# A plain last unit, earlier global values, and filler products of a constant tile in an attention and mixture-of-experts kernel

## The chip, the core and the metric

The kernel runs on one core of one Trainium2 chip. A core has a matrix engine (TensorE, PE in the profile; PEld is its weight load), a vector engine (VectorE, DVE), a scalar engine (ScalarE, ACT), a general engine (GpSimd, POOL), a queue that only issues transfers (SyncE, SP), and 16 DMA engines that move data between memory (DRAM) and the on-chip memories: SBUF for operands, PSUM for the matrix engine's results. Each engine works through its own instructions in order and waits on semaphores for the others. The metric is the time of one execution on the device in microseconds (us); lower is better.

## What is computed

First an attention over 8 batches of 8 heads with 512 local and 32 global positions of 64 values each. Global queries see all positions; local queries see the global positions and a band of 32 to each side. Then a mixture of experts over the 4352 resulting rows of 512: the logits of 8 experts go through 8 rounds of row and column scaling, and every row goes through every expert.

```python
    s_g = scale * np.matmul(q_g, k_all.transpose(0, 1, 3, 2))
    out_g = np.matmul(sm(s_g), v_all)
    ...
    s_l = np.concatenate([s_lg, s_ll], axis=-1)          # s_ll masked to |i - j| <= 32
    out_l = np.matmul(sm(s_l), np.concatenate([v_g, v_l], axis=2))
    ...
    for e in range(E):
        h = np.maximum(x @ w1[e], 0.0)
        ye = h @ w2[e]
        out += P[:, e:e + 1] * ye
```

## The kernel before

The whole program is one function, and the order of instructions on each engine is the order in which the function calls them (the schedule is manual). It has three stretches that matter here.

**The head (about 0 to 21 us).** Lines 269 to 319 load what the first batch needs. POOL issues, in this order: qs and ks of heads 2 and 3 (L174, from load_qk), four mask instructions (L310), qs and ks of heads 4 to 7 (L174), then load_v(0): the cast of the global values, cast_vg(0) (L183), which writes v_g[0] as 16-bit numbers to the DRAM tile vg16[0]; the local values va in four loads (L193, and L196 three times) and vb in one (L200). Then come cast_vg(1) (L183) and clear_z(0) (L297, L298, L300, L301), which clears the tile vgz[0], writes a column of it, and prepares vgn. SP issues load_vz(0): four loads from vg16[0] into vgz[0] (L180), each with 32 rows, and a fifth into vgn (L319). A vgz load must wait for the cast to land and for the clear. The local values are needed twice, in va and shifted in vb; for the first two batches POOL makes vb by copies (function part, L204 to L209), issued in slot 1.

**The slots.** A loop over s (L562 on) runs one slot for each of 32 pairs of heads, two heads a slot. Slot s makes the scores of pair s in three parts (st_B: PE L368, or L372 and L375 later; VectorE L379 masks and takes the minimum, ScalarE L382 the exponential), transposes the weights of pair s-1 (st_D1 L389, st_D2 L403; the copies to SBUF are VectorE's L391 and ScalarE's pg, L405), transposes the queries and keys of pair s+1 (st_A: PE L332; VectorE copies the keys into kTe, four tiles in turn, L336; ScalarE copies the queries, L337), and multiplies the weights by the values (st_E: PE L423, which reads va, vb and vgz; VectorE L427 and L428 divide and so release the PSUM tile). st_E(0) stands in slot 2, st_E(1) and st_E(2) in slot 3, and st_E(s-1) in slot s after that. Even slots from 2 on make scores of global queries (st_G1, L455), odd ones from 3 on use them (L468, L481, L494, L497). From slot 5 on the same loop also runs the first expert products of experts 0 and 1 (PE ph L523, py L537), four and two pieces a slot. In slots 1 to 4, where there is no such piece yet, keep_busy(3) follows st_A: three products of the identity with the first 512 columns of kTe[0], whose result nobody reads (L553). kTe[0] is written by st_A(0), and again by st_A(4) in slot 3.

**The experts.** Experts 2 to 7 use Strassen's scheme with seven products of half size in place of eight. The second layer works in units of 256 rows. A Strassen unit has four sums of its inputs (sums, L867, 128x512 each), seven products m1 to m7 (mm, L871, four matmuls of 256 columns each) on a PSUM tile z of four quarters (two such tiles exist), two ScalarE copies within z (L885 behind m1, L892 behind m6), and three VectorE reads into the output rows (read, L905): r2 after m4 and m5, r7, and r1 after m3. A plain unit (function plain) has 16 matmuls of 512 columns (L940) in two halves and two VectorE reads (L943); plain(u, last, between) runs the functions in between ahead of given matmuls, keyed by half and place; with last true the second half is split in three pieces of columns. Its results are in tiles of the PSUM pools mm and sc. store issues the output rows on SP (L833).

The end of the program has four units u0 to u3 behind the last Strassen unit x of the loop:

```python
        u1.sums()
        plain(u0, False, {(0, FT - 2): (x.m3, x.r1, lambda: u2.sums(nc.gpsimd)), (1, 3): (u1.m1,)})
        for w in (u1.m7, u1.m2, u1.m6, u2.m1, u1.m4, u1.m5, u1.r2, u1.r7, u2.m7, u2.m2, u2.m6, u1.m3, u1.r1):
            w()
        plain(u3, True, {(0, 3): (u2.m4, u2.m5, u2.r2, u2.r7), (0, FT - 2): (u2.m3, u2.r1)})
```

So u1 and u2 are Strassen units, u0 and u3 plain ones; u1's sums are VectorE's and u2's GpSimd's.

Of the kernel before, what the change touches and what calls it, by code (L numbers as in the profile page):

```python
# [10 lines left out]
FP16 = mybir.dt.float16  # L11
# [12 lines left out]
def kernel(  # L24
# [13 lines left out]
    nc = tc.nc  # L38
# [5 lines left out]
    P = 128  # L44
# [8 lines left out]
    FT = F // P  # L53
# [15 lines left out]
    ones_f = persist.tile([P, P], FP32)  # L69
    identity = persist.tile([P, P], FP16)  # L70
# [58 lines left out]
    with ExitStack() as att:  # L129
# [12 lines left out]
        kTe = [att_c.tile([P, KC * W], FP16, name=f"kTe{i}") for i in range(4)]  # L142
# [9 lines left out]
        def natural(b):  # L152
            return b < 2
# [18 lines left out]
        def load_qk(b, *hs):  # L172
            staged[b] = tuple(att_in.tile([P, H, NJ, Dh], FP16, tag=t, name=t) for t in ("qs", "ks"))
            return [lambda t=t, src=src, h0=h0, h1=h1: nc.gpsimd.dma_start(  # L174
                        out=t[:, h0:h1], in_=src[b, h0:h1].rearrange("h (p s) d -> p h s d", s=NJ))
                    for h0, h1 in zip(hs, hs[1:]) for t, src in zip(staged[b], (q_l, k_l))]

        def load_vz(b):
            for i in range(4):
                nc.sync.dma_start(out=vgz[b % 2][i:P:4, i, :, 0:Dh], in_=vg16[b])  # L180

        def cast_vg(b):
            nc.gpsimd.dma_start(out=vg16[b], in_=v_g[b].rearrange("h g d -> g h d"))  # L183

        def load_v(b):
            va, vb = vab[b % 2]
            vz = vgz[b % 2]
            src = v_l[b].rearrange("h s d -> s h d")

            def first():  # L190
                if b != 1:
                    cast_vg(b)
                nc.gpsimd.dma_start(out=va[W:P, 0, :, 0:Dh], in_=src[0:96])  # L193

            def mid(j):
                nc.gpsimd.dma_start(out=va[:, j, :, 0:Dh], in_=src[P * j - W : P * j + 96])  # L196

            def last():
                r = HB if natural(b) else W
                nc.gpsimd.dma_start(out=vb[r : r + W, NJ - 1, :, 0:Dh], in_=src[Sl - W : Sl])  # L200

            def part(eng, lo):
                if lo:
                    eng.tensor_copy(out=vb[96:P, NJ - 1], in_=va[W : 2 * W, 0])  # L204
                    eng.tensor_copy(out=vb[0:HB, 0:2], in_=va[HB:P, 0:2])
                    eng.tensor_copy(out=vb[0:HB, 2:NJ], in_=va[HB:P, 2:NJ])
                else:
                    eng.tensor_copy(out=vb[HB:P, 0:2], in_=va[0:HB, 1:3])
                    eng.tensor_copy(out=vb[HB:P, 2], in_=va[0:HB, 3])  # L209

            def move():
                if natural(b):
                    return part
                nc.sync.dma_start(out=vb[96:P, NJ - 1], in_=va[W : 2 * W, 0])
                nc.sync.dma_start(out=vb[0:W, :], in_=va[HB : HB + W, :])
                nc.sync.dma_start(out=vb[HB : HB + W, :], in_=va[HB + W : P, :])
                nc.sync.dma_start(out=vb[W:HB, 0 : NJ - 1], in_=va[0:W, 1:NJ])
                nc.sync.dma_start(out=vb[HB + W : P, 0 : NJ - 1], in_=va[W:HB, 1:NJ])
                load_vz(b)

            return [first] + [lambda j=j: mid(j) for j in range(1, NJ)] + [last, move]
# [38 lines left out]
        def run(steps):  # L260
            for f in steps:
                f()
# [14 lines left out]
        steps = load_qk(0, 2, 4, H)  # L277
# [18 lines left out]
        def clear_z(i, eng):  # L296
            eng.memset(vgr[i].bitcast(mybir.dt.uint32), 0)  # L297
            eng.tensor_copy(out=vgz[i][:, :, :, Dh], in_=own.unsqueeze(2).to_broadcast([P, 4, H]))  # L298
            if i == 0:
                eng.memset(vgn[0 : P - Sg], 0.0)  # L300
                eng.memset(vgn[P - Sg : P, :, Dh:VW], 1.0)  # L301
# [5 lines left out]
        for a in range(2):  # L307
            band = mask[HB * a : HB * (a + 1), 1, 0:KW]
            for base, m, c in ((0, -1, 1), (2 * W, 1, -1)):
                nc.gpsimd.affine_select(out=band, in_=band, compare_op=ALU.is_ge, fill=NEG, base=base,  # L310
                                        pattern=[[c, KW]], channel_multiplier=m)
        run(steps[2:4])
        *steps, move = load_v(0)
        part = move()
        run(steps)
        cast_vg(1)
        clear_z(0, nc.gpsimd)
        load_vz(0)
        nc.sync.dma_start(out=vgn[P - Sg : P, :, 0:Dh], in_=vg16[0])  # L319

        st = {}
# [227 lines left out]

        def keep_busy(n):  # L550
            pm = ps_mm.tile([P, 512], FP32, tag="mm", name="pm")
            for i in range(n):
                nc.tensor.matmul(pm, identity, kTe[0][:, 0:512], start=True, stop=True)  # L553

        queue = []
        NU = B * HP
# [13 lines left out]
        for s in range(NU + 2):  # L570
            b, hp = divmod(s, HP)
# [89 lines left out]
            if 1 <= s < 5:  # L661
                keep_busy(3)
# [98 lines left out]
    with tc.tile_pool(name="tpool", bufs=2) as tpool, \  # L761
# [68 lines left out]
        def store(m, c, eng):  # L830
            if m < B:
                r0 = S * m + Sg + P * c
                eng.dma_start(out=out[r0 : r0 + P, :], in_=ogs[m][:, c, :])  # L833
            else:
                for b in range(4 * c, 4 * c + 4):
                    eng.dma_start(out=out[S * b : S * b + Sg, :], in_=ogs[m][W * (b % 4) : W * (b % 4 + 1), c, :])
# [15 lines left out]
        class Unit:  # L852
# [6 lines left out]
            def o(self, j):  # L859
                return acc_of(self.m)[:, self.c[j], :]  # L860

            def sums(self, eng=nc.vector):
                a11, a12, a21, a22 = self.a
                s = self.s = hsum.tile([P, 3, HF, P], FP16, tag="hs", name="hs")
                for o, x, y, op in ((s[:, 1], a11, a21, ALU.subtract), (a21, a21, a22, ALU.add),
                                    (s[:, 0], a21, a11, ALU.subtract), (s[:, 2], a12, s[:, 0], ALU.subtract)):
                    eng.tensor_tensor(out=o, in0=x, in1=y, op=op)  # L867

            def mm(self, o, lhs, rhs, first):
                for fk in range(HF):  # L870
# [3 lines left out]
            def w(self, i, j):  # L874
                return w2s[self.k][:, HF * i : HF * (i + 1), H2 * j : H2 * (j + 1)]
# [55 lines left out]
        def plain(u, last, between):  # L931
            order = sorted(range(FT), key=lambda fk: (fk % HF == HF - 1, fk))
            for j in range(2):
                for d0, d1 in ((0, H2), (H2, 3 * P), (3 * P, D)) if last and j else ((0, D),):
                    pool, tag = (ps_sc, "sc") if (j + (d0 > 0)) % 2 else (ps_mm, "mm")
                    z = pool.tile([P, D], FP32, tag=tag, name="zp")
                    for n, fk in enumerate(order):
                        for f in between.get((j, n), ()) if d0 == 0 else ():
                            f()
                        nc.tensor.matmul(z[:, d0:d1], u.a[2 * j + fk // HF][:, fk % HF, :], work["last"][:, fk, d0:d1],  # L940
                                         start=(n == 0), stop=(n == FT - 1), skip_group_check=True)
                    o = u.o(j)[:, d0:d1]
                    nc.vector.scalar_tensor_tensor(out=o, in0=z[:, d0:d1], scalar=u.p[j], in1=o, op0=ALU.mult, op1=ALU.add)  # L943
                store(u.m, u.c[j], nc.sync)
# [135 lines left out]
        for k, (pas, e) in enumerate(stages):  # L1080
# [3 lines left out]
            n = len(slots)  # L1084
# [31 lines left out]
        p, x = state["slot"], state["unit"]  # L1116
        for w in (x.m4, x.m5, x.r2, x.r7, p.m4, p.m3):
            w()
        u0, u1, u2, u3 = final
        u1.sums()  # L1120
        plain(u0, False, {(0, FT - 2): (x.m3, x.r1, lambda: u2.sums(nc.gpsimd)), (1, 3): (u1.m1,)})
        for w in (u1.m7, u1.m2, u1.m6, u2.m1, u1.m4, u1.m5, u1.r2, u1.r7, u2.m7, u2.m2, u2.m6, u1.m3, u1.r1):
            w()
        plain(u3, True, {(0, 3): (u2.m4, u2.m5, u2.r2, u2.r7), (0, FT - 2): (u2.m3, u2.r1)})


# [28 lines left out]
```

## Time and profile before

| | |
|---|---|
| median of 3 runs (lowest, highest) | 996.84 us (996.23, 996.92) |
| the profiled execution, and its span | 996.39 us, 994.6 us |
| PE busy, matmuls | 978.8 us (98%), 8644 |
| VectorE busy | 776.9 us (78%) |
| ScalarE busy | 659.8 us (66%) |
| GpSimd busy | 305.2 us (31%) |
| mean granted PE clock | 0.998 |

The span runs from the first instruction of the program to the last event that the profile shows; the execution's own time is 1.8 us longer. All times of the text are from the span's start. Busy time counts each engine's instructions; PE's ends are modelled, about 0.17 us past the point at which the next matmul can start. "Idle before" in a timeline row is in brackets, with the instruction that ended it. A row of the chain of waits has its start, its length and the instruction, or "issue" where nothing that the profile shows was waited for. A row of a DMA issue gives the issuing queue; its landing is taken from the tile's view, issue by issue. The granted clock is 1.00 at full speed and 0.50 at half.

### The profile page before, as it was taken

The numbers are of one execution on the slowest core, as the hardware profiler recorded it, in microseconds if no ns is written. First come the engines' busy times: TensorE is split into PE (matmuls) and PEld (weight loads), VectorE is DVE, ScalarE is ACT, GpSimd is POOL, SyncE is SP. The second block draws the span as 40 slices with busy tenths as digits, with TensorE's granted clock in tenths as the row PEclk, the third lists the DMA queues.
The fourth block names the chain that finished last, engine by engine and source line by source line (L and its number), as shares of the span: only waits on it lengthen the run. The fifth ranks groups of instructions, "written<-read, shape, count | busy, mean of one in ns | idle before, by whom it ended". The sixth has DMA issues, their size and how long they took to land.

```text
span 994.6 us, 22109 instructions
## 1 busy us (share of the span) xinstructions
PE 978.8 (98%) x8644; PEld 637.0 (64%) x8644; DVE 776.9 (78%) x1919; ACT 659.8 (66%) x1372; POOL 305.2 (31%) x366
## 2 busy tenths in 40 slices
PE   7899999999999999999999999999999999999997
PEld 5565556555555556666666666676767676766765
DVE  7876666666663755899999888997899999888887
ACT  6898888888884566765555555557765555555551
POOL 9649887887860201111111111101111111100001
PEclk9999999999999999999999999999999999999999
DMA  9999999999952477554443333575654543123043
GB/s 165 189 163 207 226 213 212 224 203 234 225 141 85 121 229 189 161 138 118 117 106 75 75 74 75 138 212 138 160 138 118 117 116 71 38 56 73 2 106 128
DMA packets 138248, 138.65 MB, mean 139 GB/s; under 512 B 56800, under 2 KB 110240, under 8 KB 136096
## 3 DMA queue, kind: packets, MB, share of 16 engines
q0 software_dynamic: 105696, 87.32, 51.6%
q1 hardware_dynamic: 31888, 49.60, 15.7%
q8 instruction: 67, 1.10, 0.4%
q10 hardware_dynamic: 560, 0.33, 0.1%
q14 instruction: 37, 0.30, 0.1%
HBM read 144.46 MB, written 39.58 MB: 185 GB/s over the span
## 4 chain that ended last, share of the span: by engine, by line
PE 93%; DVE 2%; ACT 2%; POOL 1%; DMA 1%; issue 1%; SPq 0%; ACTq 0%; DVEq 0%; POOLq 0%
PE z L871 30%; PE pa L969 18%; PE py L537 12%; PE ph L523 11%; PE pb L969 9%; PE pc L969 4%; PE sc L375 1%; PE po L423 1%; PE ptw L389 1%; ACT Pu L382 1%; PE pk L332 1%; DMA vgz<-vg 1%; PE tgx L399 1%; PE pq L332 1%; PE sg L455 0%
## 5 line engine op out<-in xcount | busy, mean ns | idle before, releaser
L871 PEld LDWEIGHTS <-hs 128*128 128x128 f16 x2320 | 226.1, 98 | 96.1 <-issue 2.9
L871 PE MATMUL z<-w2e,hs 128*128 128x256 f16 x1336 | 200.4, 273 | 2.3 <-DVE o L905 1.0
L871 PE MATMUL z<-v,hs 128*128 128x256 f16 x984 | 147.6, 273 | 0.0
L892 ACT COPY z<-z 128x256 f32<-128x256 f32 x100 | 35.7, 357 | 145.9 <-PE z L871 145.9
L523 PE MATMUL ph<-xT,w1e 128*128 128x512 f16 (+1 forms) x576 | 130.2, 367 | 0.6 <-ACT xT L407 0.6
L537 PE MATMUL py<-w2e,hT 128*128 128x512 f16 x544 | 128.2, 379 | 0.0
L382 ACT ACTIVATE Pu<-ms,mx 128x160 f16<-128x160 f32 x256 | 119.6, 637 | 11.7 <-DVE mx L379 9.6
L969 PEld LDWEIGHTS <-w1e 128*128 128x128 f16 x960 | 87.1, 98 | 51.6 <-issue 1.0
L969 PE MATMUL pa<-t,s 128*128 128x512 f16 x384 | 114.2, 379 | 0.0
L787 POOL DMA_DIRECT2D w1e<-in_moe_w_dram x24 | 17.4, 733 | 290.7 <-PE pa L969 220.4
L379 DVE CUSTOM_DVE_ANT_0 ms<-sc,mask 128x160 f32<-128x160 f32 x256 | 70.0, 320 | 46.3 <-ACT yst L540 27.6
L867 DVE TENSOR_TENSOR hs<-hs 128x512 f16<-128x512 f16 x228 | 99.1, 435 | 8.4
L905 DVE SCALAR_TENSOR_TENSOR oy<-z,lg,oy 128x512 f32<-128x512 f32 x128 | 95.8, 748 | 7.3 <-ACT oy L910 5.9
L787 POOL DMA_DIRECT2D w2e<-in_moe_w_dram x24 | 19.8, 830 | 243.6 <-PE z L871 214.2
L973 DVE CUSTOM_DVE_ANT_0 hx<-pb,s 128x512 f16<-128x512 f32 x96 | 65.9, 686 | 36.4 <-ACT s L1003 30.4
L523 PEld LDWEIGHTS <-w1e 128*128 128x128 f16 x576 | 54.5, 98 | 53.0 <-issue 1.1
L989 ACT ACTIVATE hs<-pa 128x512 f16<-128x512 f32 x96 | 57.2, 596 | 46.8 <-PE pa L969 46.8
L973 DVE CUSTOM_DVE_ANT_0 hs<-pb,s 128x512 f16<-128x512 f32 x96 | 65.8, 686 | 24.1 <-ACT s L1003 23.7
L969 PEld LDWEIGHTS <-s 128*128 128x128 f16 x720 | 65.6, 98 | 28.5 <-issue 0.3
L537 PEld LDWEIGHTS <-hT 128*128 128x128 f16 x544 | 49.9, 98 | 51.9
L528 DVE TENSOR_SCALAR hT<-ph 128x512 f16<-128x512 f32 x58 | 40.1, 691 | 50.1 <-PE ph L523 50.0
L526 ACT ACTIVATE hT<-ph 128x512 f16<-128x512 f32 (+1 forms) x86 | 50.7, 589 | 27.6 <-PE ph L523 27.1
(203 smaller groups left out, 1935.0 us busy)
## 6 DMA issues: line engine op xcount, KB each, us to landing
ys<-yd SPq DMA_DIRECT2D x68, 256.0 KB, 3.2
yd<-yst SPq DMA_DIRECT2D x16, 1024.0 KB, 6.4
pw<-in_moe_w_dram POOLq DMA_DIRECT2D x24, 512.0 KB, 10.1
kept<-psum POOLq DMA_DIRECT2D x24, 512.0 KB, 4.8
s<-kept POOLq DMA_DIRECT2D x12, 768.0 KB, 8.8
v<-kept POOLq DMA_DIRECT2D x12, 768.0 KB, 8.7
w1e<-in_moe_w_dram POOLq DMA_DIRECT2D x12, 512.0 KB, 5.4
w2e<-in_moe_w_dram POOLq DMA_DIRECT2D x12, 512.0 KB, 6.5
```

Source lines behind the costliest of these rows:

```text
L379: nc.vector.tensor_tensor_reduce(out=ms[:, ii, :], in0=sc[:, SW * ii : SW * (ii + 1)], in1=mask[:, mi, :], scale=-scale, scalar=BIG, op0=A ...
L382: nc.scalar.activation(out=d["Pu"][:, i // 4, :, i % 4], in_=ms[:, ii, :], func=AF.Exp, scale=-1.0, bias=d["mx"][:, i : i + 1])
L523: nc.tensor.matmul(ph[:, 0:n], wts[e][0][:, dk, P * fm : P * (fm + 1)], xT[:, dk, c0 : c0 + n], start=(dk == 0), stop=(dk == DP - 1))
L526: nc.scalar.activation(out=hT[:, fm, 0:n], in_=ph[:, 0:n], func=AF.Relu)
L528: nc.vector.tensor_scalar(out=hT[:, fm, 0:n], in0=ph[:, 0:n], scalar1=0.0, scalar2=None, op0=ALU.max)
L537: nc.tensor.matmul(py, hT[:, fk, P * c : P * (c + 1)], wts[e][1][:, fk, :], start=(fk == 0), stop=(fk == FT - 1))
L867: eng.tensor_tensor(out=o, in0=x, in1=y, op=op)
L871: nc.tensor.matmul(o, lhs[:, fk, :], rhs[:, fk, :], start=(first and fk == 0), stop=(fk == HF - 1), skip_group_check=True)
L905: nc.vector.scalar_tensor_tensor(out=o, in0=z, scalar=p, in1=o, op0=ALU.mult, op1=ALU.add)
L969: nc.tensor.matmul(o, lhs[:, dk, P * f : P * (f + 1)], rhs[:, dk], start=(first and n == 0 and dk == 0), stop=(dk == HD - 1), skip_group_c ...
L973: nc.vector._custom_dve(TENSOR_ADD_SAT, out=self.to(i, j), in0=self.of(ps), in1=self.of(s), s0=BIG, s1=0.0)
L989: nc.scalar.activation(out=self.to(1, 0), in_=self.of(self.pa), func=AF.Relu)
```

## The change

It has three parts.

- **The end.** u2 becomes a plain unit: its sums on GpSimd, its seven products and three reads go, and 16 matmuls of 512 columns and two reads come. u1's m4, m5, r2, r7 and its m3, r1 are now called from inside u2, and u3 has nothing between its matmuls. sums loses its parameter for the engine.
- **The start.** cast_vg(0) is issued ahead of qs and ks of heads 4 to 7, no longer in load_v(0); clear_z(0) right after the first va load, ahead of the other three; load_vz(0) ahead of cast_vg(1), which is on another queue.
- **The unread products.** keep_busy(3) issues six products of 256 columns instead of three of 512; they read ones_f, a 128x128 tile of 32-bit ones taken as 256 columns of 16-bit numbers, in place of kTe[0]. ones_f is written at the start of the program (L281, and one column by L284) and never again.

```diff
             def first():
-                if b != 1:
+                if b > 1:
                     cast_vg(b)
                 nc.gpsimd.dma_start(out=va[W:P, 0, :, 0:Dh], in_=src[0:96])
...
+        cast_vg(0)
         run(steps[2:4])
         *steps, move = load_v(0)
         part = move()
-        run(steps)
+        steps[0]()
+        clear_z(0, nc.gpsimd)
+        run(steps[1:])
+        load_vz(0)
         cast_vg(1)
-        clear_z(0, nc.gpsimd)
-        load_vz(0)
         nc.sync.dma_start(out=vgn[P - Sg : P, :, 0:Dh], in_=vg16[0])
...
         def keep_busy(n):
             pm = ps_mm.tile([P, 512], FP32, tag="mm", name="pm")
-            for i in range(n):
-                nc.tensor.matmul(pm, identity, kTe[0][:, 0:512], start=True, stop=True)
+            for i in range(2 * n):
+                nc.tensor.matmul(pm[:, 0 : 2 * P], identity, ones_f.bitcast(FP16), start=True, stop=True)
...
-            def sums(self, eng=nc.vector):
+            def sums(self):
...
-                    eng.tensor_tensor(out=o, in0=x, in1=y, op=op)
+                    nc.vector.tensor_tensor(out=o, in0=x, in1=y, op=op)
...
-        plain(u0, False, {(0, FT - 2): (x.m3, x.r1, lambda: u2.sums(nc.gpsimd)), (1, 3): (u1.m1,)})
-        for w in (u1.m7, u1.m2, u1.m6, u2.m1, u1.m4, u1.m5, u1.r2, u1.r7, u2.m7, u2.m2, u2.m6, u1.m3, u1.r1):
+        plain(u0, False, {(0, FT - 2): (x.m3, x.r1), (1, 3): (u1.m1,)})
+        for w in (u1.m7, u1.m2, u1.m6):
             w()
-        plain(u3, True, {(0, 3): (u2.m4, u2.m5, u2.r2, u2.r7), (0, FT - 2): (u2.m3, u2.r1)})
+        plain(u2, False, {(0, 3): (u1.m4, u1.m5, u1.r2, u1.r7), (1, 3): (u1.m3, u1.r1)})
+        plain(u3, True, {})
```

In the order of the built program nothing else moves. In the kernel after, lines behind L313 of before have a number higher by two, those of the last units (from about L1125) by three.

## The prediction

> **What bounds the kernel now.** I read the page first, then the chain of work that ended last at both ends of the span, then the timelines of the engines there, and last the times at which single loads landed.
>
> ```profile
> PE 978.8 (98%) x8644; PEld 637.0 (64%) x8644; DVE 776.9 (78%) x1919; ACT 659.8 (66%) x1372; POOL 305.2 (31%) x366
> ...
> PE   7899999999999999999999999999999999999997
> ```
>
> TensorE (PE) is busy 98% of the span; only the first two of 40 slices and the last one leave it room. After its idle of 0.56 us at 40.05 us its timeline up to 62 us names one gap, of 0.18 us, and the chain is nearly PE alone until 972 us. So a change pays only by starting that full stretch sooner or by shortening the end. The chain near the start (start, length, what):
>
> ```profile
> 14.61 6.71 DMA vgz<-vg
> 21.32 0.04 issue
> 21.36 0.53 PE po L423 x21
> ...
> 25.75 0.61 DVE kTe L336
> 26.36 0.04 issue
> 26.40 0.81 PE pm L553 x3
> 27.21 0.30 PE sc L368 x8
> ```
>
> The first value product of slot 2 (st_E(0), L423) stops for the fourth vgz load, and in slot 3 the unread products (keep_busy, L553) stop for VectorE's (DVE's) copy into kTe[0], which is one of their operands; the scores behind them stop too. At the end, VectorE and PE:
>
> ```profile
> 970.33 0.42 DVE L867 TENSOR_TENSOR hs<-hs,hx 128x512 f16<-128x512 f16 x1
> ...
> 976.49 4.45 DVE L867 TENSOR_TENSOR hs<-hs 128x512 f16<-128x512 f16 x4
> 980.87 0.74 DVE L905 SCALAR_TENSOR_TENSOR oy<-z,lg,oy 128x512 f32<-128x512 f32 x1
> ```
> ```profile
> 976.93 5.02 POOL L867 TENSOR_TENSOR hs<-hs 128x512 f16<-128x512 f16 x4 [29.22 <-DVE hs L867]
> ```
> ```profile
> 981.66 0.60 PE L871 MATMUL z<-w2e,hs 128*128 128x256 f16 x4 [0.97 <-DVE oy L905]
> ...
> 984.76 0.60 PE L871 MATMUL z<-w2e,hs 128*128 128x256 f16 x4 [0.32 <-DVE ox L905]
> ...
> 988.51 0.60 PE L871 MATMUL z<-w2e,hs 128*128 128x256 f16 x4 [0.98 <-DVE o L905]
> 988.94 2.36 PE L940 MATMUL zp<-w2e,hs 128*128 128x512 f16 x26
> ```
>
> Four sums on VectorE take 1.8 us at 970 us, but 4.45 us at 976 us, where GpSimd (POOL) makes u2's four sums beside them. The read behind them (r1, L905) frees the PSUM tile that u2.m1 needs, so PE stands still; it does so twice more, at u1.m3 and u2.m3, for reads that come just ahead of them.
>
> **The end, step by step.** A Strassen unit is 7 products of 4 matmuls of 256 columns; four of them take 0.435 us (1.31 us for 12 in the chain), so 7 x 0.435 = 3.05 us. A plain unit is 16 matmuls of 512 columns at 0.2165 us (0.65 us for 3 in the chain) = 3.46 us. u2 as a plain unit costs 0.41 us more on PE. What goes are the three stalls, counted from where PE could have issued: 980.10 + 0.435 = 980.54 to 981.66 is 1.12; 983.84 + 0.435 = 984.28 to 984.76 is 0.48; 986.72 + 0.65 = 987.37 to 988.51 is 1.14; together 2.74 us. Net 0.41 - 2.74 = **-2.3 us**.
>
> What is late next? u1.m6 still ends its issue at 980.54, and u2's first three matmuls follow (its PSUM buffers are long free) to 981.19. u1.m4 then waits for ScalarE's (ACT's) copy of m6's result: before, it starts 0.64 us after m6 starts and takes 0.36, so 980.10 + 1.00 = 981.10: 0.09 us to spare, the tightest place. u1.m5 ends at 982.23, r2 reads until 983.0; u1.m3, which that read releases, comes at 983.79, behind five matmuls of u2's first half and three of its second. u2 ends its issue at 985.32, u3's first half at 987.05, and its three last pieces, 1.77 us as before (991.31 - 0.17 - 989.37), at 988.82; the last result is there at 989.0 against 991.31. VectorE has u1's sums in 1.8 us (978.3), then r1, and stays ahead also if they kept their 4.45: no PE instruction that is left waits for that r1. The last L943 and store (991.34 to the span's end) follow unchanged. Bounds: -1.9 (some 0.2 us each at m4 and m3) to -2.4.
>
> **The start, step by step.** On POOL's queue vg[0]'s cast moves ahead of two loads (qs and ks of heads 4 to 7), and clear_z(0), 11.27 to 13.24, moves ahead of va's three loads, to about 7.3 to 9.25. Nothing is added, so from 13.15 on POOL stands as before; the casts and loads it is moved past are issued later: qs and ks by 0.66 us (the cast's issue), the va loads and vb by 1.95, vg[1] by 1.95. On SP's queue the four vgz loads wait for the cast's landing (before: issued 5.86, 6.6 us to landing, 12.47) and for the clear's copy (12.63); before, both end together, so both had to move. After: the loads land in order of issue, ks's first part at 7.6, so the cast at about 8; the clear's copy ends near 8.65. The vgz loads then go out at 8.7 instead of 12.65, and with the same 4.6 to 6.7 us to landing the fourth is there at about 17.4, not 21.32. The next condition of st_E(0) is vb: POOL's last copy (L209) ends at 20.57. PE starts at 20.35, so it runs through and ends near 21.1 instead of 21.89; VectorE is free at 21.14. **-0.75 us**; nothing below that, for vb holds it.
>
> The copies on POOL (L204 on, from 16.20) need va, whose last two loads landed at 14.9 and 16.0, 6.7 and 7.0 us after their issue; a small cast issued at 50.7, with little queued ahead, landed 2.3 us later. Some 4 us of that are queue, so a pause of 1.95 us in issuing is covered. If that cover is gone: L206 (17.86) may wait, and each us it waits is lost to st_E(0).
>
> keep_busy: six matmuls of 256 columns cost what three of 512 do (6 x 0.109 against 3 x 0.2165 = 0.65 us). They read a tile last written at 3.64 us, so the wait in slot 3 goes and none is added; in slots 1, 2 and 4 the row shows no wait to lose. In slot 3, with the 0.75 already won: transposes from 24.34, keep_busy from 24.91 (0.35 us after pq, as in slot 2), scores from 25.65, VectorE's next L379 at 26.14 instead of 27.63: 1.49 in all. The next limit is ScalarE's copy pg (26.41 to 26.87, now 0.75 sooner, 26.12), which st_E(2) needs: its end moves by 1.3, not 1.5. ScalarE then runs with one gap of 0.24 us from 30.5 to 40.0 and starts PE's full stretch, so **-1.3 us** carries on. The loads that do not move with it land in time: vgz[1] by 36.7 for its use near 40, w2e at 49.9 for 58. Bounds: 0 (all lost to late loads) to -1.5 (pg no limit).
>
> **Sum.** -2.3 - 1.3 = -3.6 us. The profiled execution took 996.39 (span 994.6): 992.8. The three runs' median is 0.45 above it, so I forecast **993.2**.
>
> [...] In the rows, ks lands at 12.17 and its transposes start at 13.01: 0.84 to spare. The cast ahead of it costs 0.30 (its landing behind ks's now, 12.17 to 12.47). [...]
>
> **Rivals.**
> - *Shared DMA engines eat the start* (0.15). In rows: two vgz landings are 0.50 apart (17.25, 17.75); with the cast's 0.30 ks lands up to 1.3 later, 13.47, and slot 1 up to 0.46 late: the start gives -0.8. If va is held up as well by over 1.84 us (it needs to be there at 17.86), all of the start goes: 996.84 - 2.3 = 994.5. For: the GB/s at 10 to 15 us are lower (147) than at 5 to 10 (200). Against: in 17 to 20 us, with vgz loads under way, qs and ks still land 1.5 us apart.
> - *The end gives nothing* (0.05): something holds u1.m4 or u1.m3 as long as the three stalls did; 995.5. The copy's 0.09 us speaks for a little of it, the order of PE's work against.
> - *The change doesn't do what it says* (0.04): the clear or the cast is not what held vgz, and the sums' reader not what held PE: 996.8.
> - *Slower* (0.06): products of this constant tile do not count as work and the clock drops. The windows view, columns PE, PEld, DVE, ACT, POOL, clock, DMA share, GB/s:
>
> ```profile
> 7.55:10.96 3.41, 1.52 (x39) 1.02 (x36) 3.32 (x19) 3.17 (x9) 3.41 (x5) 1.00 1.53 187
> 10.96:14.37 3.41, 3.41 (x49) 2.43 (x44) 2.96 (x14) 3.10 (x8) 3.25 (x7) 0.50 2.87 145
> 14.37:17.79 3.42, 3.21 (x61) 2.18 (x59) 2.63 (x15) 2.73 (x8) 3.32 (x5) 1.00 1.56 150
> 17.79:21.20 3.41, 2.41 (x44) 1.59 (x43) 2.85 (x13) 3.12 (x8) 3.35 (x5) 1.00 1.60 204
> ```
>
> A stretch with 1.52 us of PE was followed by 3.41 us at clock 0.50; with 2.41 or more it stayed at 1.00. Work done at half clock overruns its stretch by twice its busy time less 3.41: up to 3.0, 1.4, 2.9, 1.5, 1.8 and 2.0 us for the six from 14.37 to 34.85, 12.6 together: 1005.8. From the second such stretch on it outweighs the 3.6. Against: the products at 1.33 read a tile of zeros (L279, L267), and the clock was 1.00 from 4.13 on.
>
> [...]
>
> **How the numbers follow.** Forecast 0.70; the rivals as given, 0.15, 0.05, 0.04, 0.06. Low end: -1.5 - 2.4 on 996.84 is 992.9, less the runs' spread of 0.7: 992.2. High end: only the end's smaller bound, -1.9, 994.9, and 0.3 of spread: 995.2. About 0.2%, 2.0 us, is what a measurement of this kernel can tell from no change: under 994.85 is faster. That takes the forecast and 0.13 of the first rival: 0.83; slower is the clock's 0.06; the rest, 0.11, is the same.
>
> **What would show it.** Right: no idle of PE before L423 in slot 2 and L368's first VectorE reader in slot 3 about 1.3 to 1.5 us earlier; PE's ph (L523) at about 38.8; no PE gap of 0.3 us or more after 975; VectorE's sums 0.43 us each; from the last L940 result to the first p.m3 2.3 us less. Wrong: PE idle before L332 in slot 1, POOL idle before L206, clock 0.50 in a second stretch, or a new wait at u1.m4.

## The result, and the profile after

The changed kernel takes 994.55 us (median of 11 runs, 993.18 to 995.89); the kernel before, on the same chip, 997.0 (11 runs, 996.23 to 999.38). The ratio is 0.9972, 95% interval 0.9963 to 0.9981: some 2.8 us less (1.9 to 3.7). The forecast was 3.6 less. The profiled execution of the kernel after took 994.4 us (span 992.6), 2.0 less than that of before.

The page of the kernel after, engines and then PE in 40 slices:

```profile
PE 981.9 (99%) x8644; PEld 639.0 (64%) x8644; DVE 773.6 (78%) x1918; ACT 659.4 (66%) x1370; POOL 300.6 (30%) x362
...
PE   8899999999999999999999999999999999999998
```

The first and the last slice are each one tenth fuller. PE's 3.1 us of added busy time are more than u2's 0.41: the rest is work at half clock at the start, as will be seen (up to 39 us PE is busy 32.95 us, where it was 30.07).

The end. VectorE's timeline of the kernel after, then PE's:

```profile
976.79 1.88 DVE L869 TENSOR_TENSOR hs<-hs 128x512 f16<-128x512 f16 x4
978.59 0.74 DVE L907 SCALAR_TENSOR_TENSOR oy<-z,lg,oy 128x512 f32<-128x512 f32 x1
```
```profile
984.15 0.60 PE L873 MATMUL z<-w2e,hs 128*128 128x256 f16 x4
984.58 4.74 PE L942 MATMUL zp<-w2e,hs 128*128 128x512 f16 x37
```

u1's four sums take 1.88 us in place of 4.45, r1 follows at 978.59, and no PE row after 975 has a bracket with a wait any more. From the start of the first plain matmul of the end (zp) to the end of the last one it is 14.12 us, against 16.41: 2.29 less, where 2.3 were forecast.

The start. The chain of the kernel after in slot 3, then PE's timeline (its unread products in slots 1 and 2, the first value product of st_E(0), the first transposes of slot 3), then POOL's:

```profile
26.23 0.22 PE pq L334 x8
26.46 0.76 PE pm L555 x6
27.22 0.28 PE sc L370 x8
```
```profile
14.74 1.46 PE L555 MATMUL pm<-ones_f,identity 128*128 128x256 f16 x6
...
20.57 0.83 PE L555 MATMUL pm<-ones_f,identity 128*128 128x256 f16 x6
...
21.91 0.22 PE L425 MATMUL po<-va,pw 128*64 128x65 f16 x1
...
25.82 0.41 PE L334 MATMUL pk<-identity,ks 128*64 128x128 f16 x8 [0.18 <-ACT pgs L472]
```
```profile
18.57 1.05 POOL L206 COPY vb<-va 64x1040 f16<-64x1040 f16 x1 [0.68 <-DMA va<-in_v_l_dram]
...
20.68 0.62 POOL L209 COPY vb<-va 64x520 f16<-64x520 f16 x1
```

The unread products of slot 3 start as soon as the transposes are through; VectorE's copy is gone from the chain. But slot 3 comes late: its transposes start at 25.82, not at the 24.34 of the forecast. The six products took 1.46 us in slot 1 and 0.83 in slot 2, so PE was still at half clock in slot 1 (to 17.39, where the clock's records start). st_E(0) starts at 21.91 (before 20.35) and runs without a stop; the fourth vgz load had landed at 18.24. POOL's copy L206 waited 0.68 us for the last va load, as the first rival had it, so that vb was complete at 21.3 instead of 20.6; but that is still ahead of st_E(0), so in this execution it cost nothing.

The prediction's sign "ph at about 38.8" meant the ph that ends PE's idle at 40.05 in the profile of before; it comes at 40.29, not at 38.8. Below, ph is the first of them, at 38.67 before.

By place, after less before: the start up to this first ph +0.23 us (38.90 against 38.67), the middle (from there to the end's first zp) +0.08, the end with what follows it -2.31; together -2.0, the difference of the two spans. The profile thus shows the end's gain whole and none of the start's 1.3.

### The profile page after: what moved, and what is told of

It is laid out like the page before. It is cut to its first block, busy times and chain, and to the rows that moved or that the text cites. A ratio compares the mean times of both kernels' runs of the same rounds, so it can differ in the third digit from the quotient of the medians.

```text
span 992.6 us, 22100 instructions
## 1 busy us (share of the span) xinstructions
PE 981.9 (99%) x8644; PEld 639.0 (64%) x8644; DVE 773.6 (78%) x1918; ACT 659.4 (66%) x1370; POOL 300.6 (30%) x362
## 3 DMA queue, kind: packets, MB, share of 16 engines
q1 hardware_dynamic: 31888, 49.60, 15.4%
## 4 chain that ended last, share of the span: by engine, by line
PE 95%; ACT 3%; DVE 1%; issue 0%; ACTq 0%; DVEq 0%
PE z L873 31%; PE pa L971 18%; PE py L539 12%; PE ph L525 11%; PE pb L971 9%; PE pc L971 4%; ACT Pu L384 1%; PE po L425 1%; PE ptw L391 1%; PE sc L377 1%; PE zp L942 1%; PE pk L334 1%; PE pq L334 1%; PE tgx L401 1%; PE sg L457 0%; DVE ms L381 0%
## 5 line engine op out<-in xcount | busy, mean ns | idle before, releaser
L873 PEld LDWEIGHTS <-hs 128*128 128x128 f16 x2292 | 223.4, 98 | 93.1 <-DVE hs L869 0.5
L873 PE MATMUL z<-w2e,hs 128*128 128x256 f16 x1320 | 198.0, 273 | 0.0
L789 POOL DMA_DIRECT2D w1e<-in_moe_w_dram x24 | 17.4, 732 | 292.7 <-PE pa L971 220.4
L869 DVE TENSOR_TENSOR hs<-hs 128x512 f16<-128x512 f16 x228 | 96.6, 424 | 8.4
```

The source lines that it names most:

```text
L869: nc.vector.tensor_tensor(out=o, in0=x, in1=y, op=op)
L873: nc.tensor.matmul(o, lhs[:, fk, :], rhs[:, fk, :], start=(first and fk == 0), stop=(fk == HF - 1), skip_group_check=True)
```

## The experiments

Three theories were set against each other. *Pause* (in the expectations with the shared DMA engines): va's loads land late, and take the start's gain back. *Clock*: how long PE stays at half clock at the start differs from execution to execution, and the profile of before was a lucky one. *Cover*: as forecast, both gains are there. Each part was first run alone. The experiments ran on three chips, each beside runs of the kernel before on the same chip, and each is compared with those.

**The end alone** (before, with the new end; nothing moved at the start).

> The end alone (u2 a plain unit), start and unread products as before. Theory 1, as forecast: -2.3 us against before (bounds -1.9 to -2.4), no PE gap of 0.3 us or more after 975 us, VectorE's last sums 0.43 us each. Theory 2, the end is where the forecast overshot: less than -1.5 us, with a new PE gap at u1.m4 or u1.m3.

Measured: 995.18 us (11 runs) against 997.07; ratio 0.9985, interval 0.9976 to 0.9994, some 1.5 us less (0.6 to 2.4). In the profile the end is 14.12 us again, exactly 2.29 less. The start of that execution, though, is that of the kernel before with another clock. Its windows, columns as in the prediction:

```profile
6.36:9.78 3.42, 2.28 (x53) 1.57 (x52) 2.60 (x15) 1.85 (x6) 3.42 (x5) 1.00 1.33 202
9.78:13.19 3.41, 2.15 (x32) 1.78 (x32) 2.62 (x14) 3.10 (x9) 2.94 (x6) 0.50 2.20 162
13.19:16.60 3.41, 3.41 (x35) 2.02 (x33) 1.94 (x9) 2.43 (x7) 3.36 (x6) 0.50 2.12 132
16.60:20.02 3.42, 2.63 (x65) 1.97 (x63) 3.32 (x17) 2.65 (x7) 3.30 (x4) 1.00 1.54 186
```

Half clock from 9.78 to 16.60, two windows, where the profile of before had one (10.96 to 14.38). st_E(0) starts at 21.64, when vgz has landed (20.68): the stop for vgz is not there, though no load was moved. In slot 3 PE's timeline of this kernel still has the other wait:

```profile
26.87 0.81 PE L553 MATMUL pm<-kTe,identity 128*128 128x512 f16 x3 [0.69 <-DVE kTe L336]
```

**The moved loads alone.**

> The start's loads alone: the cast and the clear sooner, nothing else. Forecast: -0.75 us; PE without a stop in L423 of slot 2, vgz landed by 17.5. Theory of the shared DMA engines: about 0 us (within 0.2), because the sooner vgz loads push the last va load past 17.86 us, POOL idles before L206 and st_E(0) waits for vb as long as it waited for vgz. Theory of the clock: the gain is there, but the start's half-clock stretches lie elsewhere in each execution and move single runs by more than 0.75.

Measured: 996.97 us (11 runs), ratio 1.0 (0.9991 to 1.0008): no gain is seen, though the interval, from 0.9 us less to 0.8 more, does not shut out the forecast's 0.75. POOL's timeline in the head, and PE's in slot 9:

```profile
18.87 1.05 POOL L206 COPY vb<-va 64x1040 f16<-64x1040 f16 x1 [0.99 <-DMA va<-in_v_l_dram]
```
```profile
75.41 0.19 PE L425 MATMUL po<-vgz,pg 128*64 128x65 f16 x1 [0.29 <-DMA vgz<-vg]
76.01 0.19 PE L425 MATMUL po<-vgz,pg 128*64 128x65 f16 x1 [0.41 <-DMA vgz<-vg]
```

The first row is the pause. st_E(0) starts at 21.66 all the same, with vb complete at 21.59, and runs without a stop; with the end alone, at the same clock, it started at 21.64. The other two were not forecast: st_E(8), the first to read batch 2, stops for the vgz loads of that batch, and the time from the first ph to the end's first zp grows from 936.3 to 937.4 us. The last of these loads lands at 75.97 here, and between 72.5 and 74.5 in the seven profiles in which the head's vgz loads are not moved.

**The unread products alone.**

> The unread products alone (six of 256 columns on the tile of ones). Forecast, taken alone: -0.7 us; in slot 3 no PE idle before them and VectorE's next L379 some 0.75 us sooner than 27.63 if slot 2 is as before. If constant products did not count as work, a half-clock stretch would follow slots 2 to 4 and the time would rise by 1 us or more.

Measured: 997.19 (11 runs), ratio 1.0003 (0.9995 to 1.0012). In PE's timeline slot 3's wait is gone:

```profile
26.73 0.83 PE L553 MATMUL pm<-ones_f,identity 128*128 128x256 f16 x6
```

and from VectorE's first division of st_E (L427) to its third it is 5.72 us, against 6.25 before and 6.24 with the end alone: 0.52 less, and pg (ScalarE's copy) ends last, as forecast. The timed runs do not resolve 0.5 us: the interval goes from 0.5 less to 1.2 more, with the gain just at its edge.

**The pause taken out of the way.** In the kernel after, the copies of vb that need va's last load are made last:

```diff
                     eng.tensor_copy(out=vb[0:HB, 0:2], in_=va[HB:P, 0:2])
+                    eng.tensor_copy(out=vb[HB:P, 0:2], in_=va[0:HB, 1:3])
+                else:
                     eng.tensor_copy(out=vb[0:HB, 2:NJ], in_=va[HB:P, 2:NJ])
-                else:
-                    eng.tensor_copy(out=vb[HB:P, 0:2], in_=va[0:HB, 1:3])
                     eng.tensor_copy(out=vb[HB:P, 2], in_=va[0:HB, 3])
```

> The changed kernel, with POOL's copies into vb in another order: the one that reads only va's first three parts (L208) ahead of the one that needs the last (L206). Theory of the shared DMA engines: the last va load (18.5 us in the profile of after) is covered by 1.05 us more of copies, POOL no longer idles before L206, L209 ends near 20.6 instead of 21.3, and the time falls by up to 0.7 us against after, that is -3.1 to -3.5 against before. Forecast and theory of the clock: vb is not what st_E(0) waits for, no difference to after (-2.8 against before).

Measured: 994.15 (8 runs), ratio 0.9971 (0.9961 to 0.9981), some 2.9 us less: the same as the kernel after, though the interval does not shut out the 3.1 to 3.5 of the theory of the pause. POOL no longer waits and vb is complete at 20.85. The start came out at 38.13 for ph, but its half clock also ended early (15.4), and PE's timeline has slot 9's stop:

```profile
74.41 0.19 PE L425 MATMUL po<-vgz,pg 128*64 128x65 f16 x1 [0.33 <-DMA vgz<-vg]
```

**The kernel before, once more**, to see how far its own start varies.

> The kernel before, unchanged, for another profiled execution. Theory of the clock: the first profile was an execution with little half-clock time in the start (7.5 us up to 14.4); here st_E(0) is reached at 21 us or later, the fourth vgz load (about 21) is no wait or one under 0.4 us, and ph (L523) starts 0.2 to 0.6 us later than 38.67. Theory of the shared DMA engines: this execution looks like the first one, st_E(0) at 20.4 and a stop of 0.6 us or more for vgz.

Measured (one run): 997.11 us. Half clock ends at 15.3, not 14.4; st_E(0) starts at 20.89, not 20.35; ph comes at 39.35, not 38.67. PE's row of the vgz stop:

```profile
22.04 0.19 PE L423 MATMUL po<-vgz,pg 128*64 128x65 f16 x1 [0.54 <-DMA vgz<-vg]
```

So 0.7 us of the start are one execution against another of the same kernel. Neither theory had all of it: the clock is late, and the start with it, but by its row the stop is 0.54 and not under 0.4.

**What the end's gain is made of.** First u2 stays a Strassen unit and only its sums move from GpSimd to VectorE (`lambda: u2.sums(nc.vector)`).

> The kernel before with u2's sums on VectorE in place of GpSimd, u2 still a Strassen unit. Before, the end takes 16.4 us from the first plain matmul to the last. If only GpSimd's sums slowed the end: 13.9 us or less, since PE has 0.41 us less work than after (14.1). Forecast's view, that the reads of a Strassen unit just ahead of u3 hold PE as well: the first stop (1.12 us) goes, the ones at u1.m3 and u2.m3 stay in part, 14.4 to 15.3 us.

Measured (one run): 995.96 us; the end takes 15.45 us, a little above what was expected. VectorE's sums, and PE's rows:

```profile
976.99 1.87 DVE L867 TENSOR_TENSOR hs<-hs 128x512 f16<-128x512 f16 x4
```
```profile
984.30 0.60 PE L871 MATMUL z<-w2e,hs 128*128 128x256 f16 x4 [0.32 <-DVE ox L905]
...
988.04 0.60 PE L871 MATMUL z<-w2e,hs 128*128 128x256 f16 x4 [0.98 <-DVE o L905]
```

With GpSimd idle u1's sums take 1.87 us and the first stop is gone; that is 0.96 of the 2.29. The other two stops stay; the plain unit removes them, for 1.33.

Then the other way round: the kernel after, with four sums on GpSimd where u2's had been, whose results nobody reads.

> The changed kernel with four sums on GpSimd beside u1's sums as before, their result unread (of u2's inputs none is changed). Forecast: VectorE's sums slow down to about 4.4 us again, but no PE instruction waits for the r1 behind them, so from the first L942 matmul to the last the time stays 14.1 us (within 0.1). [...]

Measured (one run): 995.09 us; the end takes 14.69 us, above the 14.1 (within 0.1) that was expected. VectorE, POOL, and PE:

```profile
976.89 4.45 DVE L869 TENSOR_TENSOR hs<-hs 128x512 f16<-128x512 f16 x4
```
```profile
977.34 5.03 POOL L1129 TENSOR_TENSOR hs<-hs 128x512 f16<-128x512 f16 x4 [29.22 <-DVE hs L869]
```
```profile
74.78 0.19 PE L425 MATMUL po<-vgz,pg 128*64 128x65 f16 x1 [0.96 <-DMA vgz<-vg]
...
984.82 0.60 PE L873 MATMUL z<-w2e,hs 128*128 128x256 f16 x4 [0.48 <-DVE ox L907]
```

The 4.45 us are back, to the hundredth: u1's four sums take 1.87 us with GpSimd idle and 4.45 beside GpSimd's four, which take 5.03. Why they take longer beside GpSimd's, no run shows. And PE stands still for 0.48 us at u1.m3, which waits for r2: r2 comes on VectorE behind the late r1 of x. The cost is 0.57 of the 2.29.

**More work for PE at the start**, to shorten the half clock: the kernel after with twelve unread products in slot 0 in place of two.

> The changed kernel with more unread products in slot 0: four in place of two behind st_A(0), two behind st_A(1), six at the end of the slot. Theory of the clock: less half-clock time before 17 us, st_E(0) reached near 20.5 in place of 21.9, its next limit is vb (20.6 to 21.3), 0.5 to 1 us faster than after on the median and less spread. If the clock is not what moves the start: no gain, or 0.3 us slower from the added products.

Measured: 995.54 (11 runs) against 997.6, ratio 0.9979 (0.997 to 0.9988). In its profile half clock lasts one window (8.80 to 12.21) and the span is 992.0, the shortest of all; over the timed runs nothing is gained on the kernel after. st_E(0) starts at 21.25 there, though the clock was full from 12.21: PE's transposes of slot 2 wait 0.80 us for VectorE's copy pw (L393), so the clock is not the only thing that sets the start. Shortening the half clock this way is not shown to help.

**Only the clear moved** (before, clear_z(0) ahead of va's last three loads; the cast, and so the vgz loads, nearly where they were: issued at 12.92).

> The kernel before with only the clear moved ahead of the last three va loads; the cast stays, so the vgz loads go out at about 12.6 as before. If the pause in POOL's issues is what makes the last va load late: it lands at 18 us or later and POOL idles before L206. If the sooner vgz loads' packets do it: it lands by 17 us and POOL does not idle there.

Measured (one run): 997.2 us. va's last load is issued at 10.90 and lands at 18.07; in the profile of before 9.04 and 16.02, in that of after 10.91 and 18.52. It is as late without a vgz load issued ahead of it, so the pause alone is enough. POOL:

```profile
18.12 1.05 POOL L206 COPY vb<-va 64x1040 f16<-64x1040 f16 x1 [0.37 <-DMA va<-in_v_l_dram]
```

**Slot 9's stop removed**: the kernel after with load_vz(b) issued ahead of the five vb loads (L214 to L218) for the later batches, and then the same with the copies in the other order as well.

> The changed kernel with one more step: from batch 2 on, the vgz loads of a batch go out on SP ahead of the five vb moves instead of behind them. Theory of the second stop (what the sooner loads win before slot 2 is partly given back in slot 9, where st_E(8) waits for vgz of batch 2, because POOL's queue runs 0.7 us or more later): PE has no idle before L425 near 74 us, and the time between the first ph and the first plain matmul is 936.3 us in this execution as in the ones without the moved loads; about -0.5 us against after, -3.3 against before. If slot 9's stop is no more than chance: no difference to after (-2.8).

> The same with POOL's copies in the order that leaves the last va load more time. Theory of the shared DMA engines and of the second stop together: POOL idles less than 0.3 us before L206, st_E(0) waits for nothing, slot 9 neither: the fastest of all, -3.3 to -3.8 us against before. Clock theory alone: as after, -2.8.

Measured: 994.1 (6 runs), 0.9963 (0.9949 to 0.9976), and 993.96 (6 runs), 0.996 (0.9945 to 0.9975). The vgz loads of batch 2 land by 62, PE has no idle time in slot 9, and the middle takes 936.35 and 936.37 us. These are the lowest medians measured, but their intervals overlap that of the kernel after: that they beat it is not shown.

**The end and the unread products without the moved loads.**

> The changed kernel without the moved loads (the end and the unread products alone). Theory of the second stop and the shared engines, by which the moved loads bring nothing on the median: as after, -2.8 us against before (-2.3 and -0.5). Forecast: 0.75 us slower than after, -2.0.

Measured: 994.71 (12 runs), 0.9971 (0.9963 to 0.998). The kernel after has 0.9972. The moved loads, a third of the diff, bring nothing that the runs can tell. (The profiled execution was the slowest of the twelve: half clock to 19.7, st_E(0) at 23.38.)

## Why the prediction was right or wrong

**The end, -2.3: right in size and cause.** 16.41 to 14.12 in each profile with the new end unaltered. u1.m4 did not wait. The side claim that the end would hold even with sums of 4.45 us was wrong: I followed r1 to its own reader, and not r2 behind it in VectorE's order, for which u1.m3 waits (0.48). The timed runs with the end alone gave 1.5 less, and their interval holds 2.3.

**The unread products, -0.55: right, by the profiles.** 0.52 less between st_E's divisions, with pg as the next limit. The slower rival is out: in all the profiles with these products the clock stays full from the end of the start's half clock until PE's work ends (1.00 from 17.39 to the span's end in the kernel after's). So constants are not seen to count less than data.

**The moved loads, -0.75: this is the step that failed,** in three places. The timed runs do not shut 0.75 out; the profiles show where it went.

First, the stop itself. I took 0.8 us from one execution and set it against the median of the runs. The stop depends on when st_E(0) starts, which mostly follows the end of the half clock, and on when the last vgz load lands, which varies by 1.7 us with nothing moved. The last column is the time from st_E(0)'s first product to VectorE's first division, less the 0.74 us that it takes without a stop:

| run | full clock from | st_E(0) starts | last vgz landed | its stop |
|---|---|---|---|---|
| before | 14.4 | 20.35 | 21.32 | 0.82 |
| before again | 15.3 | 20.89 | 22.00 | 0.96 |
| the end alone | 16.6 | 21.64 | 20.68 | 0 |
| sums on VectorE | 16.6 | 21.62 | 20.91 | 0 |
| only the clear moved | 17.4 | 21.90 | 21.94 | 0 |
| unread products alone | 17.55 | 21.93 | 22.40 | 0.33 |
| end and products | 19.7 | 23.38 | 21.46 | 0 |
| *vgz moved:* unread sums on GpSimd | 15.1 | 20.65 | 17.26 | 0.14 (vb) |
| *vgz moved:* the other copy order | 15.4 | 21.15 | 16.63 | 0 |
| *vgz moved:* the moved loads alone | 16.6 | 21.66 | 17.37 | 0 |
| *vgz moved:* the kernel after | 17.4 | 21.91 | 18.24 | 0 |

Where the clock comes late, vgz is there in time or nearly, and there is little or nothing to win. At an equal clock it can be read directly: "only the clear moved" and the kernel after both reach full clock at 17.4 and start st_E(0) at 21.90 and 21.91; ph comes at 39.40 and 38.90, and the 0.50 between them is the unread products' 0.52. Where the clock comes early, the start's gain is there as forecast: with full clock from 15.1 to 15.4, ph comes at 37.77 and 38.13 with the moved loads and the products, and at 39.35 in "before again", 1.6 and 1.2 less. But in these same two executions the middle gives 1.2 and 0.5 back, by the third place below. The moved loads did land sooner, at 16.6 to 18.4 in the seven profiles with them, where 17.4 was forecast. The prediction's sign, no idle of PE before the value products of slot 2, says little by itself: it is met by the end alone too, where no load was moved.

Second, "a pause of 1.95 us in issuing is covered". It is not: the last va load, issued some 1.9 us later, lands between 17.9 and 18.8 in the eight profiles with the clear moved, and between 16.0 and 17.2 in the five others that record it. It takes 6.8 to 8.2 us at either place; I had read 4 of those 7 us as a queue that would empty during the pause. POOL's idle before L206, one of the prediction's signs of being wrong, is there (0.68 in the kernel after's profile). But the late vb costs st_E(0) next to nothing: 0.14 us in the profile with the unread sums, none in the others of the table. The first rival had the place right (L206, and vb behind it). Its time, 994.5, was met by luck, for it has all of the start lost to va. Its mechanism, vgz loads ahead of va's on the shared DMA engines, is not needed, for va is as late without them. The first rival also had ks land up to 1.3 us later, at 13.47; ks's second part landed at 12.1 to 12.8 in the profiles with the early vgz loads and at 11.6 to 12.6 in the others, so no such loss is seen.

Third, "the loads that do not move with it land in time" named vgz[1] and w2e and left out vgz of batch 2. With moved loads its last load lands at 73.8 to 76.0 in five profiles (73.78 in the kernel after's own), without them at 72.5 to 74.5 (wanted at 74.3 or later), while st_E(8) of those five wants it at 73.5 to 74.8. In three of the five PE stopped, and the middle grew by 0.5 to 1.2 us; in the kernel after's own profile and in that with more work at the start it did not. Issued earlier, the stop is gone. The two ranges of landing overlap, so that the moved loads make it late is likely and not shown; how the head's order would reach a load 50 us later was not settled.

**The sum.** -2.29 - 0.52 = -2.81, beside the measured 2.8 (1.9 to 3.7); the loads' 0.75 is what was too much. This division rests on the profiles. By their ratios the parts run alone took 1.5 less, the same, and 0.3 more, together 1.2 less; intervals of some 0.9 us to either side of each still allow 2.8, but do not show how it divides. Of the three theories *Clock* fits best: the pause costs hardly anything, and the forecast's cover holds for the end, for the products, and for the loads only where the clock came early.

**Open:** what makes a window one of half clock, and why va's loads keep their 7 us when they are issued later.

## What to carry to other kernels

A stop at the start that is seen in one profile should be looked for in a second profile of the same kernel before it is priced: here it was 0.8 to 1.0 us when the clock came early, and 0 to 0.3 when it came late. When work is put into a queue that issues transfers, count the transfers behind it as late by all of that work (here the last va load, issued at 10.91 in place of 9.04, landed at 18.52 in place of 16.02), and look at each load of that queue by its user's time, also far down the program. And a stall behind an engine's queue is followed through every later instruction of that engine, not only through the one that waits first.

## What was not expected of the hardware

- In the ten profiles whose clock records begin before 7 us, the stretch of half clock that follows begins anywhere from 8.45 to 11.69 us, and lasts 3.41 us or two or three times that. Counted in windows of that length from its edges, how busy PE was does not quite settle it: a window at full clock with 2.38 us of PE was followed by half clock (sums on VectorE, from 6.33), one with 2.32 was not (the end alone, from 30.26). At half clock, a window with 2.15 us of PE was followed by another (the end alone, from 9.78), and those with 3.41 by full clock.
- In the kernel after's profile the clock reads 1.00 up to its first record, at 17.39, though the products of slot 1 took 1.46 us there, against 0.83 in slot 2, and the first eight transposes, at 4.86, 0.64 against 0.41 in the profile of before; the length of an instruction of known size is the safer reading.
